# Decode attention with a gated feed-forward: the last weight loads cut into pieces of 4, 5, 2 and 1 blocks, the third split by partition

## The chip, the cores and the metric

The kernel runs on one core of a Trainium2 chip. The metric is device microseconds of one execution. One further execution was recorded by the hardware profiler, and all rows below are from that one.

## The reference, cut to what matters

```python
x = A_x                                            # [2, 1, 448]
g = sigmoid((x * gate_w).sum(-1, keepdims=True))
# attention for one new token: 16 heads of 256, 4096 cached keys, all float32
q = (x @ wq)  -> [2, 16, 1, 256]
p = softmax(q . k_cache * 256 ** -0.5)
a = (p . v_cache) -> [2, 1, 4096] @ wo             # wo: [4096, 448]
# feed-forward
h = relu(x @ w1 + b1) ** 2                         # w1: [448, 1792]
b = h @ w2 + b2                                    # w2: [1792, 448]
return g * a + (1 - g) * b                         # [2, 1, 448]
```

The caches k and v are 128 MiB each, and w2 is 1792 x 448 float32, 3.2 MB.

## The kernel before, in words

Work goes in 16 rounds. A round is one batch row and two heads; its keys are two loads of 4 MB (`load_k`), its values one load of 8 MB (`load_v`, L148). VectorE multiplies the keys by q (`times_q`, L305) and sums rows (`row_sums`, L310); TensorE multiplies the softmax weights with the values (`values`, L355). Keys, the last half of the values and all weights share a ring of three SBUF slots (tag `ring`), and the other values use one wide slot. All large loads are issued by SyncE (SP), in program order, on one DMA queue; a load into a slot waits until the last reader of the tile before it is done. The schedule is manual: each engine keeps the order in which the program is written.

w2 is viewed as `w2_v`, 128 partitions of 14 blocks (`FC`) of 448 float32, so that a partition's 14 blocks lie one behind the other in DRAM and a block is 1,792 bytes of one partition. The first two blocks (`WH`) are loaded early. The other 12 go into the ring's slot that the last half of the last keys leaves (`load_w2_late`), as the last loads of the program. Before the change they are four loads, cut at `W2_CUTS = (4, 8, 11)`: pieces of 4, 4, 3 and 1 blocks, each over all 128 partitions.

The end of the program, as TensorE executes it: the last values (`va`, then three pieces of `vb`), `take` and `turn` of the last two heads, `late_w2(0, 4)` with the first piece, `late_wo` of two heads (L405), then `late_w2(4, 12)` with the pieces left. A block of w2 is four matmuls in `late` (L401), in the trace eight records; they add up in the PSUM tile `fin`. ScalarE copies `fin` to `y4` (L504), and two small stores, one issued by SP (L506) and one by ScalarE (L507), write the output of 4 rows each.

The small loads at the start are issued by ScalarE: `x2`, `gw` and `b2r` of 2 rows each, and `b1T` of 128 rows.

Of the kernel before, what the change touches and what calls it, by code (L numbers as in the profile page):

```python
# [16 lines left out]
def kernel(  # L17
# [14 lines left out]
    nc = tc.nc  # L32
    P = 128
# [17 lines left out]
    assert QB == 2 * DH  # L51
    DQ = D // 4
    WH = 2
    W2_CUTS = (4, 8, 11)
    V_CUTS = (48, 56)
    LEAD = 4
    LEAD2 = 16
# [32 lines left out]
    w2_v = w2.rearrange("(p c) n -> p c n", c=FC)  # L90
    w2_sb = {}

    def w2_slot(lo, hi):
        t = slot(f"w2_{lo}")
        tv = t[:, :(hi - lo) * D].rearrange("p (c n) -> p c n", n=D)
        for c in range(lo, hi):
            w2_sb[c] = tv[:, c - lo, :]
        return tv
# [5 lines left out]
    def load_w2_late():  # L104
        tv = w2_slot(WH, FC)
        at = [0, *W2_CUTS, FC - WH]
        for lo, hi in zip(at, at[1:]):
            nc.sync.dma_start(tv[:, lo:hi, :], w2_v[:, WH + lo:WH + hi, :])

# [259 lines left out]
    def turn(u):  # L371
        n = len(units[u])
        pt = ps.tile([P, 512], F32, name=f"ot{u}", tag="sm")
        wide = n == HG
        nj = HJ if wide else NJ
        if wide:
            ov = o_w.rearrange("r s j k p -> r s j (k p)")
        else:
            ov = o_sb[u].rearrange("r (s p j) -> r s j p", s=2, j=nj)
        ptv = pt[:, :nj * n * B].rearrange("p (j c) -> p j c", c=n * B)  # L380
        for j in range(nj):
            for s in range(2):
                nc.tensor.matmul(ptv[:, j, :], ov[:, s, j, :], rl_t[u][:, :, s], start=(s == 0), stop=(s == 1))  # L383
        if wide:

            oT[u] = work.tile([P, HJ, B], F32, name=f"oT{u}", tag="oTw")
            for k in range(n):
                at = slice(k * HP, (k + 1) * HP)
                nc.scalar.activation(oT[u][at], ptv[at, :, B * k:B * k + B], AF.Copy)  # L389
        else:  # L390
            oT[u] = work.tile([P, NJ, n * B], F32, name=f"oT{u}", tag=f"oT{n}")
            nc.scalar.activation(oT[u], ptv, AF.Copy)
# [10 lines left out]
    def late_wo(h):  # L403
        u, k = unit_of[h]
        for j in range(NJ):  # L405
            late(oT[u][:, j, B * k:B * k + B], wo_sb[NG - 1][:, h % HG, j, :])

    def late_w2(lo, hi):
        for c in range(WH + lo, WH + hi):
            late(hT[:, c, :], w2_sb[c], stop=(c == FC - 1))  # L410
# [17 lines left out]
    for i, (b, n) in enumerate(rounds):  # L428
# [15 lines left out]
        if i == last:  # L444
            load_w2_late()
# [52 lines left out]
    turn(NG)  # L498
    late_w2(0, W2_CUTS[0])
    late_wo(H - 2)  # L500
    late_wo(H - 1)
    late_w2(W2_CUTS[0], FC - WH)
    y4 = const.tile([P, DQ], F32, name="y4")
# [31 lines left out]
```

## Time and profile before

| | us |
|---|---|
| median of 3 runs (lowest, highest) | 682.23 (681.94, 682.29) |
| the profiled execution, its own time | 682.01 |
| its span, first to last instruction | 680.2 |

The span covers 3,769 instructions. By its page DMA moves 289.79 MB at a mean of 426 GB/s, VectorE is busy for 571.7 us (84% of the span) and TensorE for 242.5 us (36%). The own time is 1.8 us above the span.

### The profile page before, as it was taken

Reading aid. Unit: us, or ns where it says so; the run is one execution under the profiler, and the core shown is the slowest. Engines: PE = TensorE matmul, PEld = TensorE weight load, DVE = VectorE, ACT = ScalarE, POOL = GpSimd, SP = SyncE. Lnnn points to the kernel's source line nnn. Section 1 sums busy time; section 2 is a strip of 40 time slices with the busy share of each in tenths; the row PEclk is TensorE's granted clock in tenths of the full one; section 3 lists DMA queues with packets and bytes.
Section 4 is the critical chain, followed back from the end, with each engine's and each line's share of the span. In section 5 each row is a group of like instructions: output and inputs, shape, how many; then the busy total and the mean of one; then the engine's idle time right before and its main releaser. Section 6 shows DMA issues by size and latency. Waiting matters only on the chain.

```text
span 680.2 us, 3769 instructions
## 1 busy us (share of the span) xinstructions
PE 242.5 (36%) x1618; PEld 85.2 (13%) x1618; DVE 571.7 (84%) x171; ACT 35.5 (5%) x110; POOL 0.7 (0%) x6
## 2 busy tenths in 40 slices
PE   2500506208158050504028450320506814033356
PEld 1100101005014010101004110000101400001013
DVE  3199999597987979799895979979796897999960
ACT  0100000100001000000001000000001000001000
POOL 0000000000000000000000000000000000000000
PEclk9955856758566685756657875575857757557779
DMA  9999999999999999999999999999999999999996
GB/s 379 436 459 414 429 461 405 448 418 426 456 405 455 407 431 443 421 447 418 445 419 436 449 413 447 416 447 418 444 438 411 449 422 432 446 414 430 413 430 265
DMA packets 9644, 289.79 MB, mean 426 GB/s; under 512 B 1174, under 2 KB 1308, under 8 KB 2332
## 3 DMA queue, kind: packets, MB, share of 16 engines
q1 hardware_dynamic: 9464, 289.54, 99.0%
q8 instruction: 12, 0.20, 0.1%
q10 hardware_dynamic: 164, 0.02, 0.0%
q14 instruction: 4, 0.03, 0.0%
HBM read 289.56 MB, written 0.00 MB: 426 GB/s over the span
## 4 chain that ended last, share of the span: by engine, by line
DMA 56%; DVE 26%; PE 17%; ACT 1%; issue 0%; SPq 0%; ACTq 0%
DMA v<-in_A_v_cache_dram 46%; PE po_buf L355 13%; DVE k L305 13%; DVE s L310 13%; DMA k<-in_A_k_cache_dram 4%; DMA wq<-in_A_wq_dram 3%; DMA w<-in_B_w_dram 3%; PE po_buf L225 1%; PE acc L396 1%; PE ot L383 1%; ACT shared L365 0%; PE fin L401 0%; ACT oT L389 0%; PE pq L262 0%; ACT qs L251 0%
## 5 line engine op out<-in xcount | busy, mean ns | idle before, releaser
L305 DVE TENSOR_TENSOR k<-k,q 128x4096 f32<-128x4096 f32 (+3 forms) x63 | 281.6, 4486 | 78.2 <-DMA k<-in_A_k_cache_dram 59.2
L310 DVE TENSOR_REDUCE s<-k 128x32 f32<-128x8192 f32 x32 | 278.0, 8686 | 1.1
L355 PE MATMUL po_buf<-v,pw 128*16 128x512 f32 (+1 forms) x960 | 137.2, 735 | 159.2 <-DMA v<-in_A_v_cache_dram 159.2
L318 PE MATMUL mt<-ident,m 128*64 128x64 f32 x64 | 7.3, 316 | 236.9 <-DVE m L314 236.9
L355 PEld LDWEIGHTS po_buf<-v,pw 128*16 128x16 f32 (+1 forms) x960 | 30.7, 111 | 254.2 <-issue 205.4
L318 PEld LDWEIGHTS mt<-ident,m 128*64 128x64 f32 x64 | 4.8, 190 | 244.4 <-issue 201.5
L329 ACT ACTIVATE pw<-s,nb 64x64 f32<-64x64 f32 x32 | 11.1, 348 | 275.0 <-DVE nb L324 274.7
L396 PE MATMUL acc<-wo,oT 128*2 128x448 f32 x48 | 23.4, 651 | 2.5 <-ACT oT L389 2.5
L383 PE MATMUL ot<-rl,shared 128*128 128x8 f32 x96 | 20.3, 350 | 5.2 <-ACT shared L365 5.2
L383 PEld LDWEIGHTS ot<-rl,shared 128*128 128x128 f32 x96 | 19.7, 314 | 8.3 <-ACT shared L365 8.3
L265 ACT ACTIVATE q<-pq 128x256 f32<-128x256 f32 x16 | 6.1, 384 | 196.0 <-PE pq L262 195.9
L262 PE MATMUL pq<-qs,ident 128*64 128x256 f32 x64 | 10.7, 419 | 0.7 <-ACT qs L251 0.7
L225 PE MATMUL po_buf<-wq,xT 128*4 128x512 f32 x56 | 8.3, 761 | 4.9 <-DMA wq<-in_A_wq_dram 4.9
L365 ACT ACTIVATE shared<-po_buf 128x1024 f32<-128x1024 f32 x6 | 5.8, 1020 | 55.8 <-PE po_buf L355 55.8
L286 PEld LDWEIGHTS pt<-ident,shared 4*128 4x128 f32 x28 | 6.9, 336 | 0.9 <-issue 0.9
L286 PE MATMUL pt<-ident,shared 4*128 4x4 f32 x28 | 7.0, 380 | 0.0
L396 PEld LDWEIGHTS acc<-wo,oT 128*2 128x2 f32 x48 | 4.4, 96 | 19.3 <-issue 16.5
L329 ACT ACTIVATION_READ_ACCUMULATOR pw<-s,nb 64x1 f32 x32 | 5.9, 185 | 0.0
L335 PE MATMUL sum<-rs,ones_pp 128*128 128x8 f32 (+1 forms) x10 | 3.0, 369 | 8.1 <-ACT pw L329 8.1
L355 PE MATMUL po_buf<-va,pw 128*8 128x512 f32 x32 | 5.2, 804 | 1.0 <-DMA va<-in_A_v_cache_dram 1.0
L225 PE MATMUL ph<-w,xT 128*4 128x448 f32 x28 | 5.4, 539 | 0.0
L262 PEld LDWEIGHTS pq<-qs,ident 128*64 128x64 f32 x64 | 3.3, 138 | 11.6 <-issue 9.7
(64 smaller groups left out, 60.8 us busy)
## 6 DMA issues: line engine op xcount, KB each, us to landing
k<-in_A_k_cache_dram SPq DMA_DIRECT2D x32, 4096.0 KB, 30.9
v<-in_A_v_cache_dram SPq DMA_DIRECT2D x2, 4096.0 KB, 28.9
wq<-in_A_wq_dram SPq DMA_DIRECT2D x1, 7168.0 KB, 19.7
wo<-in_A_wo_dram SPq DMA_DIRECT2D x4, 1792.0 KB, 34.0
va<-in_A_v_cache_dram SPq DMA_DIRECT2D x1, 4096.0 KB
w<-in_B_w_dram SPq DMA_DIRECT2D x1, 3136.0 KB
vb<-in_A_v_cache_dram SPq DMA_DIRECT2D x1, 2048.0 KB
vb<-in_A_v_cache_dram SPq DMA_DIRECT2D x2, 1024.0 KB, 16.8
```

The costliest lines, as they stand in the source:

```text
L225: nc.tensor.matmul(out[32 * g:32 * g + 2 * B, :width], xT[:, half, c].rearrange("p s b -> p (s b)"), t[:, (a * n + g) * width:(a * n + g + ...
L262: nc.tensor.matmul(pq[k * PH:(k + 1) * PH, :DH], ident[:, r:r + 1].to_broadcast([P, PH]), qs[:, k * DH:(k + 1) * DH], start=True, stop=True)
L265: nc.scalar.activation(q_sb[i], pq[:, :DH], AF.Copy)
L286: nc.tensor.matmul(pt[:, c, :], hv[:, c, :], ident[:2 * B, :2 * B], start=True, stop=True)
L305: nc.vector.tensor_tensor(kt, kt, q_sb[i].unsqueeze(1).to_broadcast([P, hi - lo, DH]), op=ALU.mult)
L310: nc.vector.tensor_reduce(s_t[i][:, half * J:(half + 1) * J], kts[i, half], axis=AX.X, op=ALU.add)
L318: nc.tensor.matmul(mt[at, :PH], m.to_broadcast([P, PH]), ident[:, at], start=True, stop=True)
L329: nc.scalar.activation(pw[k, b][at, :, 2 * c:2 * c + 2], s_t[i][at].rearrange("p (m s) -> p m s", s=2), AF.Exp, bias=nb[at], accum_out=rs_ ...
L355: nc.tensor.matmul(po[r:r + 4 * n, :], pw[k, b][:, m, :4 * n], vt[:, 2 * m:2 * m + 2, :].rearrange("p j d -> p (j d)"), start=(k == 0 and ...
L365: nc.scalar.activation(o_w[:, s], po_bufs[u % 2][:, s * DH:(s + 1) * DH].rearrange("r (p j) -> r j p", j=HJ).unsqueeze(2).to_broadcast([P, ...
L383: nc.tensor.matmul(ptv[:, j, :], ov[:, s, j, :], rl_t[u][:, :, s], start=(s == 0), stop=(s == 1))
L396: nc.tensor.matmul(acc[:, :D], oT[g][:, j, :], wo_sb[g][:, j, :], start=False, stop=(g == NG - 2 and j == HJ - 1))
```

## The change

The cuts become (4, 9, 11): pieces of 4, 5, 2 and 1 blocks. The third piece is issued as three loads that differ in their partitions: 0 to 63, 64 to 114 and 115 to 127, which is 64, 51 and 13 partitions. All bytes stay the same; six loads are issued where there were four. The order of TensorE's work is not touched.

```diff
     WH = 2
-    W2_CUTS = (4, 8, 11)
+    W2_CUTS = (4, 9, 11)
+    W2_ROWS = (64, 115)
     V_CUTS = (48, 56)
...
         at = [0, *W2_CUTS, FC - WH]
         for lo, hi in zip(at, at[1:]):
-            nc.sync.dma_start(tv[:, lo:hi, :], w2_v[:, WH + lo:WH + hi, :])
+            rows = [0, *(W2_ROWS if lo == W2_CUTS[1] else ()), P]
+            for p, e in zip(rows, rows[1:]):
+                nc.sync.dma_start(tv[p:e, lo:hi, :], w2_v[p:e, WH + lo:WH + hi, :])
```

## Rows read from the trace of the kernel before

**Rows 1.** The page: DMA packets in sum, and the chain that ended last.
```profile
DMA packets 9644, 289.79 MB, mean 426 GB/s; under 512 B 1174, under 2 KB 1308, under 8 KB 2332
...
DMA 56%; DVE 26%; PE 17%; ACT 1%; issue 0%; SPq 0%; ACTq 0%
```

**Rows 2.** The chain that ended last, from 655 us: start us, us, what.
```profile
647.50 8.70 DVE s L310
...
656.59 0.43 SPq L108
...
657.07 18.76 DMA w<-in_B_w_dram
...
675.87 0.99 PE fin L401 x32
...
676.89 0.26 ACT y L504
```

**Rows 3.** Windows at the end: us, busy by engine, clock, share of 16 DMA engines, GB/s.
```profile
670.00:672.00 2.00, 1.67 (x28) 0.84 (x20) 0.00 (x0) 0.60 (x1) 0.00 (x0) 1.00 1.02 419
672.00:672.50 0.50, 0.50 (x6) 0.50 (x5) 0.00 (x0) 0.00 (x0) 0.00 (x0) 1.00 0.94 384
672.50:673.00 0.50, 0.50 (x21) 0.48 (x24) 0.00 (x0) 0.18 (x1) 0.00 (x0) 1.00 0.93 369
673.00:673.50 0.50, 0.50 (x32) 0.50 (x24) 0.00 (x0) 0.00 (x0) 0.00 (x0) 1.00 0.70 283
673.50:674.00 0.50, 0.50 (x32) 0.50 (x24) 0.00 (x0) 0.00 (x0) 0.00 (x0) 1.00 0.62 226
674.00:674.50 0.50, 0.50 (x32) 0.40 (x24) 0.00 (x0) 0.00 (x0) 0.00 (x0) 1.00 0.45 179
674.50:675.00 0.50, 0.50 (x28) 0.33 (x16) 0.00 (x0) 0.00 (x0) 0.00 (x0) 1.00 0.29 100
675.00:675.50 0.50, 0.10 (x5) 0.00 (x0) 0.00 (x0) 0.00 (x0) 0.00 (x0) 1.00 0.23 79
675.50:676.00 0.50, 0.13 (x8) 0.13 (x12) 0.00 (x0) 0.00 (x0) 0.00 (x0) 1.00 0.16 61
676.00:676.50 0.50, 0.50 (x28) 0.50 (x24) 0.00 (x0) 0.00 (x0) 0.00 (x0) 1.00 0.00 0
```

**Rows 4.** DMA from 673 to 676 us: packets, MB, share of 16 engines.
```profile
q8 instruction: 1, 0.02, 2.3%
```

**Rows 5.** Timeline of the end: start us, us, engine, line, operation (xcount), idle before.
```profile
672.60 0.95 PE L401 MATMUL fin<-w,hT 128*2 128x112 f32 x32
...
673.37 0.95 PE L401 MATMUL fin<-wo,oT 128*2 128x112 f32 x32
...
674.15 0.95 PE L401 MATMUL fin<-w,hT 128*2 128x112 f32 x32
...
675.87 0.95 PE L401 MATMUL fin<-w,hT 128*2 128x112 f32 x32 [0.77 <-DMA w<-in_B_w_dram]
```

**Rows 6.** The page's DMA queues: packets, MB, share of 16 engines.
```profile
q1 hardware_dynamic: 9464, 289.54, 99.0%
q8 instruction: 12, 0.20, 0.1%
q10 hardware_dynamic: 164, 0.02, 0.0%
```

**Rows 7.** DMA of the first 30 us: queue packets; issues xcount, KB each.
```profile
q10 hardware_dynamic: 156, 0.02, 0.4%
...
x<-in_A_x_dram ACTq DMA_DIRECT2D x1, 3.5 KB
gw<-in_gate_w_dram ACTq DMA_DIRECT2D x1, 3.5 KB
b2r<-in_B_b_dram ACTq DMA_DIRECT2D x1, 3.5 KB
b1T<-in_B_b_dram ACTq DMA_DIRECT2D x1, 7.0 KB
```

**Rows 8.** SP's issues in the timeline from 630 us.
```profile
651.09 1.28 SPq L158 DMA_DIRECT2D vb<-in_A_v_cache_dram  x3
656.22 1.75 SPq L108 DMA_DIRECT2D w<-in_B_w_dram  x4
```

**Rows 9.** What SP's queue waited for, from 640 us: total us, times, longest.
```profile
SPq L506 <- ACT y L504: 12.3, 1, 12.3
SPq L506 <- DMA vb<-in_A_v_cache_dram: 6.8, 1, 6.8
```

## The prediction

> **What bounds the kernel now.** I read the page first, then the chain backwards from the end, then the DMA engines in half microseconds around the place where the chain leaves the loads. DMA moves 426 GB/s over the whole span and holds 56% of the chain [rows 1]. All loads before the late w2 keep their order, so everything up to SP's first w2 issue at 656.22 stays. The reader should look at the last piece of the chain: SP issues the third w2 piece at 657.07, its load holds the chain for 18.76 us and lands at 657.07 + 18.76 = 675.83, TensorE starts on it at 675.87, ScalarE copies at 676.89 [rows 2]. So the end hangs on when that piece lands on the slowest of 16 DMA engines.
>
> The windows show that "slowest" matters. Up to 672 the share is 1.02, all engines busy; then it falls over almost 4 us: 0.94, 0.93, 0.70, 0.62, 0.45, 0.29, 0.23, 0.16 [rows 3]. In engines that is 15 at 672 and 0.29 x 16 = 4.6 around 674.75, 3.7 around 675.25. The last window holds 0.16 x 0.5 x 16 = 1.28 engine-us: four engines that work until about 675.8. The sum of the eight shares times 0.5 is 2.16 us, so the same bytes spread evenly would be through at 674.16, 1.7 us earlier. An even finish is thus worth at most 1.7 us, 0.25% of the run, before TensorE's own work is counted.
>
> One reason for the spread is in the rows: one engine fetched instructions in this stretch, 2.3% of 16 engines over 3 us, 1.1 us of one engine [rows 4]; there are 12 such fetches in the span [rows 6]. As the load queue never runs dry, an engine that carried one or two stays late.
>
> **The change part by part.**
>
> *Unit.* At 419 GB/s one engine moves 26.2 GB/s [rows 3]; a block of one partition (1,792 B) takes 0.0684 us. A load over 128 partitions gives each engine 8 rows.
>
> *How the split loads fall on engines.* On the queue of the small loads the page counts 164 packets [rows 6], and the first 30 us hold 156 [rows 7]. Three loads of 2 rows and one of 128 are 134 rows, which leaves 22 = 2 + 2 + 2 + 16: one closing packet for each engine used. The other 8 packets are ScalarE's store of 4 rows: 4 rows and 4 closers, so 4 engines. So rows were dealt in equal shares over as many engines as that allows. For 64 partitions that is 16 engines with 4 rows; for 13 it is 13 with 1; for 51 it is 3 with 17. No row shows an odd count, so I bound 51 rows from both sides: all on one engine, or spread over 16 at 3 or 4 each. I take three, the nearest to the rows' equal shares.
>
> The Trainium skill ("DMA: Bandwidth & Descriptors", section "Why a DMA increments its semaphore by 16 and not by 1") says so outright: as many engines, up to 16, as divide the row count, and on this path the lowest-numbered ones, so 51 rows burden engines 0 to 2. The trace agrees for 2, 4 and 128 rows; no row here shows 51 or 13.
>
> *Work per engine in units (rows x blocks).* Through the third piece, before: 8 x 11 = 88; through the fourth, 96. After, the first two pieces are 8 x 9 = 72. The third adds 2 x (4 + 17 + 1) = 44 on the three engines, 2 x 5 = 10 on ten others, 2 x 4 = 8 on the last three. Through the third piece that makes 116, 82 and 80: +28, -6 and -8 units, or +1.92, -0.41 and -0.55 us. The same differences hold through the fourth.
>
> *Landings, if the three are early engines.* For a late engine of the ten, the third piece lands at 675.83 - 0.41 = 675.42. Before, the fourth landed at about 675.83 + 8 x 0.0684 = 676.38, which nothing waited for: TensorE reached block 11 only three blocks after 675.87. After, it lands at 675.97. The second piece had landed by 674.15, where TensorE starts on it without a wait [rows 5]; with one more block it lands by 674.15 + 0.55 = 674.70.
>
> *TensorE.* Groups of four blocks start 0.77 and 0.78 us apart and end 0.95 after their start [rows 5]: 0.193 a block and 0.18 for the last to drain. From a landing to the start take 0.04 (675.83 to 675.87). Three ways to the end: from the second piece, 674.74 + 8 x 0.193 + 0.18 = 676.46; from the third, 675.46 + 3 x 0.193 + 0.18 = 676.22; from the fourth, 676.01 + 0.193 + 0.18 = 676.38. The second piece, now five blocks, is the latest. Before, the end was 675.87 + 0.95 = 676.82. Gain: 0.36 us. A landing before 674.15 for the second piece would stop the gain at 0.44, where the fourth takes over. So the 1.93 us moved onto three engines buys a third of a microsecond: TensorE's queue of eight blocks behind the second piece is what shuts off the rest.
>
> *Two more issues, and a wait.* Four issues took 1.75 us [rows 8], so two more cost some 0.9 us of SP, from 657.97 to 658.9. SP also holds issues back for older loads: after 657.97 the output store, which reads no v, waited 6.8 us for a vb load, to 664.8 [rows 9]. I count the store as the eighth issue behind the first vb piece (two vb, four w2, one store on ScalarE's queue, then this). With two more loads, the eighth behind it is the fourth w2 piece: it would go out at 664.8 to 665.2 instead of 657.5. Behind it on SP stands only the store, which has to wait for y until 677.2 anyway. The cover is the engines' backlog: all stay busy to 672, 6.8 us after the issue [rows 3]; I cost it at nothing. Without the cover each microsecond late would be a microsecond at the end.
>
> *Waiting for three loads instead of one* in front of block 9: bounded by nothing and by one more instruction on TensorE's queue, below 0.04 us; I take nothing.
>
> *Sum.* 682.01 own time - 0.36 = 681.65. The median shown lies 0.22 above that execution's own time, so 681.87; I write 681.9. A difference of 0.2% (1.36 us) is about what a measurement of this kernel can tell from no change; this one is 0.05%.
>
> **The rivals.**
>
> *A. One of the three engines is late.* An engine that takes 17 rows ends 1.92 us later. If it is one of the four late ones, the fourth piece lands at 676.38 + 1.92 = 678.30, TensorE ends at 678.30 + 0.04 + 0.37 = 678.71, 1.89 later than before: 684.1, slower by 0.28%. It decides from the point where the engine's fourth piece landed, before, later than 676.82 - 0.41 - 1.92 = 674.49 (no gain left), and by 0.2% from 675.85 on. For it: dealt blindly, three engines miss the four late ones in 12 x 11 x 10 / (16 x 15 x 14) = 39% of cases. Against it: by 674 some half of the engines are through, and following the packet records from one packet's end to the next one's start, the two engines that carried the 2-row loads at the start are in the early half at the end (no view names engines, so this is a reading without a row, and the third engine stays open). Late engine 6%; one of the middle, between 682.3 and 683.6, 10%.
>
> *B. 51 rows on one engine.* It would carry 2 x (4 + 51 + 1) = 112 units in the third piece, or 2 x 68 = 136 if the 13 rows land there too, where it had 24; with the 8 more of the second piece that is 96 to 120 units on top, 6.6 to 8.2 us. Even an engine whose fourth piece landed at 673.5 would land it at 680.1 to 681.7; TensorE would end at 680.5 to 682.1, 3.7 to 5.3 later than before: 686 to 687.5. Rows for equal shares in 2, 4 and 128 don't exclude it. 3%.
>
> *C. The change doesn't do what it says.* If 51 rows spread over 16 engines, each has 8 to 9 rows again, the fourth piece lands at 676.38 as before, TensorE now waits for it: 676.38 + 0.04 + 0.37 = 676.79, and the time stays at 682.2. The same comes out if loads of 64 partitions run at half speed: 4 rows of 2 blocks take 0.55 us more, which eats the 0.41. The Trainium skill speaks for that ("SBUF — State Buffer", section "Door 1: The DMA port swizzle"): 64 adjacent partitions reach 8 of 16 ports, so such a load gets little more than half the speed. By it the fourth piece would land at 676.5 and the time be 682.3. No row here has a load of 64 partitions; against it stands that the late engines are alone at the end. Together 14%.
>
> **How the numbers follow.** Forecast (three early engines, 681.3 to 682.1 with the spread of 0.35 us among the runs shown) 65%; C 14%, 682.0 to 682.5; A's middle 10%, to 683.6; A late 6%, 684.1; B 3%, 686 to 687.5; 2% for a gain above 1.36 us, which needs more than the even finish leaves. The range from 681.2 to 683.1 takes in the forecast, C and most of A's middle. Faster by over 0.2%: 2%. Within 0.2% (680.9 to 683.6): 65 + 14 + 10 = 89%. Slower: 6 + 3 = 9%.
>
> **What would show it.** Right: six w2 issues, the last at about 665; the DMA share near 0.9 until about 674, then a steeper fall that ends near 675.4; TensorE's last group starting before 675.87 with less than 0.2 us of waiting on w2; y at about 676.5. Wrong in distribution: share of 0.06 to 0.2 lasting beyond 676 (one to three engines with the 17 rows), TensorE waiting there. Wrong in the queue: a DMA share falling below 1 before 671, because the fourth piece was issued too late.

## The result: 0.3% slower

The changed kernel takes 684.4 us (median of 8 runs) against 682.32 for the kernel before, a ratio of 1.0031 (95% interval 1.0019 to 1.0042). Forecast was 681.9, in a range from 681.2 to 683.1. The first profiled execution of the changed kernel ran its matmuls slower (TensorE busy for 378.2 us against 240.0) and took 703.88 us, so the ratio leaves it out, and the rows here are of a second profiled execution, whose own time of 684.80 us is its series' median (run `x1_again` below).

The end of the chain, as in [rows 2] (start us, us, what), and the timeline of TensorE there, as in [rows 5]:

```profile
656.43 20.76 DMA w<-in_B_w_dram
677.19 0.04 issue
677.24 2.58 PE fin L404 x64
679.82 0.02 issue
679.84 0.26 ACT y L507
```
```profile
672.68 0.95 PE L404 MATMUL fin<-w,hT 128*2 128x112 f32 x32
673.45 0.95 PE L404 MATMUL fin<-wo,oT 128*2 128x112 f32 x32
677.24 2.56 PE L404 MATMUL fin<-w,hT 128*2 128x112 f32 x64 [2.84 <-DMA w<-in_B_w_dram]
```

The piece that comes too late is not the split one. The load issued at 656.43 is the second, whole piece; it lands at 677.19, where the forecast had 674.70. TensorE idles for 2.84 us, and then its eight blocks take 2.56 us instead of 1.72.

The windows, as in [rows 3] (us, busy by engine, granted clock, share of 16 DMA engines, GB/s; a packet counts whole in the window in which it starts, so a share can come out above 1):

```profile
670.00:671.00 1.00, 1.00 (x20) 0.35 (x17) 0.00 (x0) 0.00 (x1) 0.00 (x0) 1.00 1.04 434
671.00:671.50 0.50, 0.31 (x16) 0.05 (x4) 0.00 (x0) 0.50 (x1) 0.00 (x0) 1.00 0.99 366
671.50:672.00 0.50, 0.35 (x3) 0.35 (x4) 0.00 (x0) 0.10 (x1) 0.00 (x0) 1.00 1.07 244
672.00:672.50 0.50, 0.50 (x7) 0.50 (x6) 0.00 (x0) 0.00 (x0) 0.00 (x0) 1.00 1.03 254
...
673.50:674.00 0.50, 0.50 (x32) 0.50 (x24) 0.00 (x0) 0.00 (x0) 0.00 (x0) 1.00 0.95 219
...
676.50:677.00 0.50, 0.00 (x0) 0.00 (x0) 0.00 (x0) 0.00 (x0) 0.00 (x0) 1.00 0.42 129
677.00:677.50 0.50, 0.26 (x12) 0.27 (x16) 0.00 (x0) 0.00 (x0) 0.00 (x0) 1.00 0.34 129
677.50:678.00 0.50, 0.50 (x31) 0.50 (x24) 0.00 (x0) 0.00 (x0) 0.00 (x0) 0.93 0.12 43
678.00:678.50 0.50, 0.50 (x20) 0.45 (x15) 0.00 (x0) 0.00 (x0) 0.00 (x0) 0.50 0.00 0
...
679.50:680.00 0.50, 0.30 (x8) 0.00 (x0) 0.00 (x0) 0.16 (x1) 0.00 (x0) 0.50 0.00 0
```

Read the last two columns together. Until 671 they say 434 GB/s at a share of 1.04, 26 GB/s for each busy engine. From 671.5 the engines stay busy but move 244 GB/s at 1.07, 14 GB/s each. Before, a falling share and falling GB/s went together [rows 3]; here engines are busy and slow. The column before them, the granted clock, falls from 1.00 to 0.50 (2.4 to 1.2 GHz) at about 678, while TensorE is at work again.

### The profile page after: what moved, and what is told of

Read it like the earlier page. It is cut to its first block, busy times and chain, and to the rows that moved or that the text cites. A ratio compares the mean times of both kernels' runs of the same rounds, so it can differ in the third digit from the quotient of the medians.

```text
span 702.0 us, 3772 instructions
## 1 busy us (share of the span) xinstructions
PE 378.2 (54%) x1618; PEld 103.7 (15%) x1618; DVE 571.6 (81%) x171; ACT 35.4 (5%) x110; POOL 0.7 (0%) x6
## 4 chain that ended last, share of the span: by engine, by line
DMA 52%; PE 36%; DVE 10%; ACT 1%; issue 0%; ACTq 0%
DMA v<-in_A_v_cache_dram 49%; PE po_buf L358 32%; DVE k L308 5%; DVE s L313 5%; DMA wq<-in_A_wq_dram 3%; PE po_buf L228 2%; PE fin L404 1%; PE ot L386 1%; PE pq L265 0%; ACT pw L332 0%; ACT q L268 0%; PE sum L338 0%; ACT o L372 0%; ACT qs L254 0%; DVE nb L327 0%
## 5 line engine op out<-in xcount | busy, mean ns | idle before, releaser
L358 PE MATMUL po_buf<-v,pw 128*16 128x512 f32 (+1 forms) x960 | 225.5, 1140 | 122.3 <-DMA v<-in_A_v_cache_dram 120.6
L358 PEld LDWEIGHTS po_buf<-v,pw 128*16 128x16 f32 (+1 forms) x960 | 39.2, 140 | 281.8 <-issue 235.6
L399 PE MATMUL acc<-wo,oT 128*2 128x448 f32 x48 | 39.4, 1023 | 2.5 <-ACT oT L392 2.5
L386 PE MATMUL ot<-rl,shared 128*128 128x8 f32 x96 | 22.8, 373 | 4.9 <-ACT shared L368 4.9
L386 PEld LDWEIGHTS ot<-rl,shared 128*128 128x128 f32 x96 | 22.3, 349 | 10.9 <-ACT shared L368 10.9
L265 PE MATMUL pq<-qs,ident 128*64 128x256 f32 x64 | 17.3, 669 | 0.7 <-ACT qs L254 0.7
L228 PE MATMUL po_buf<-wq,xT 128*4 128x512 f32 x56 | 13.1, 1134 | 4.8 <-DMA wq<-in_A_wq_dram 4.8
L228 PE MATMUL ph<-w,xT 128*4 128x448 f32 x28 | 11.6, 1030 | 0.0
L358 PE MATMUL po_buf<-vb,pw 128*8 128x512 f32 x32 | 8.0, 1152 | 0.0
L358 PE MATMUL po_buf<-va,pw 128*8 128x512 f32 x32 | 7.5, 1124 | 0.0
```

What stands on the lines that cost most here:

```text
L228: nc.tensor.matmul(out[32 * g:32 * g + 2 * B, :width], xT[:, half, c].rearrange("p s b -> p (s b)"), t[:, (a * n + g) * width:(a * n + g + ...
L265: nc.tensor.matmul(pq[k * PH:(k + 1) * PH, :DH], ident[:, r:r + 1].to_broadcast([P, PH]), qs[:, k * DH:(k + 1) * DH], start=True, stop=True)
L358: nc.tensor.matmul(po[r:r + 4 * n, :], pw[k, b][:, m, :4 * n], vt[:, 2 * m:2 * m + 2, :].rearrange("p j d -> p (j d)"), start=(k == 0 and ...
L399: nc.tensor.matmul(acc[:, :D], oT[g][:, j, :], wo_sb[g][:, j, :], start=False, stop=(g == NG - 2 and j == HJ - 1))
```

## The experiments

Each is the file of the changed kernel or the one before with the edit shown; "..." marks lines left out. The ratio is to runs of the kernel before on the same chip.

**The changed kernel again, for its profile.**

> The changed kernel once more, for a profile at the usual TensorE clock. Theory L (one of the three DMA engines that take 17 rows is late, by fetched instructions, so the loads end on it): 1.5 to 2.2 us slower than before; one engine alone is busy at the end, a DMA share of about 0.06 for over half a microsecond, and TensorE waits for w2 in front of its last group. Theory P (a load of 64 partitions runs at about half speed on every engine): slower too, but the share stays at 0.2 or more until the end, several engines ending together. Theory Q (the fourth piece is issued late, behind an older load's landing): a DMA share that drops below 0.9 before 671 and comes back.

684.80 us, ratio 1.0037 (1.0023 to 1.0051), 2.5 us slower. Theory L, rival A of the forecast, comes near in size (1.5 to 2.2 us) and has the wrong picture: the share is 0.42 at 676.75, six to seven engines, not one. Theory Q is out, since the share stays at 1 until 672.5. The rows look most like P's: the share is still 0.34 from 677 to 677.5.

**The cuts alone.**

```diff
-    W2_ROWS = (64, 115)
+    W2_ROWS = ()
```

> Cuts 4, 5, 2, 1 alone, every piece over all 128 partitions. All three theories: no loss. The fourth piece now has two blocks in front of it instead of three, so 0.0 to 0.4 us faster to 0.3 us slower than before (worked out: second piece at 674.7, third 675.83, fourth 676.38, TensorE's end 676.79 against 676.82).

682.43 us, 1.0001 (0.9992 to 1.0009): the cuts neither cost nor gain anything that can be measured. The loss is in the split. The second piece, the same five blocks, lands at 675.02 here:

```profile
656.62 18.40 DMA w<-in_B_w_dram
675.02 0.04 issue
```

**The split alone.**

```diff
-    W2_CUTS = (4, 9, 11)
+    W2_CUTS = (4, 8, 11)
```

> Old cuts 4, 4, 3, 1 with the third piece, now three blocks, in loads of 64, 51 and 13 partitions. Theory L: the 17 rows are half as long again, three engines get 42 units more than before instead of 28, 2.9 us instead of 1.9: about 1.0 us slower than the changed kernel, 2.5 to 3.2 us slower than before. Theory Q: same number of loads and waits, so the same time as the changed kernel. Theory P: the 64 rows cost 0.8 instead of 0.55 us more, so some 0.3 us slower than the changed kernel.

685.67 us, 1.0051 (1.0039 to 1.0064), 0.9 us above the changed kernel. Q is out again; L (1.0) fits better than P (0.3), which stays.

**Two halves, no 51 and 13.**

```diff
-    W2_ROWS = (64, 115)
+    W2_ROWS = (64,)
```

> Cuts 4, 5, 2, 1 with the third piece in two loads of 64 partitions each; no engine carries more rows than another. Theory L: no loss, within 0.3 us of the cuts alone. Theory P: 0.5 to 1.1 us slower than the cuts alone, since all of the third piece goes through loads of 64 partitions. Theory Q: within 0.3 us of the cuts alone.

685.11 us, 1.0040 (1.0027 to 1.0052). No engine carries more rows than another, yet the loss is as large as the changed kernel's. That ends L as the main cause: the loads of 51 and 13 aren't needed for the loss. It is also more than twice what P was sized at: 2.7 us above the cuts alone instead of 0.5 to 1.1. TensorE waits twice here, for the second piece and then for the split one, and its last three blocks take 1.30 us, where 3 x 0.193 + 0.18 are 0.76:

```profile
676.67 1.14 PE L404 MATMUL fin<-w,hT 128*2 128x112 f32 x40 [2.20 <-DMA w<-in_B_w_dram]
678.82 1.30 PE L404 MATMUL fin<-w,hT 128*2 128x112 f32 x24 [1.01 <-DMA w<-in_B_w_dram]
```

**The same two halves, interleaved.** Two more theories now: S, that writing to one side of the partitions slows all engines; N, that it is the number of loads.

```diff
-            rows = [0, *(W2_ROWS if lo == W2_CUTS[1] else ()), P]
-            for p, e in zip(rows, rows[1:]):
-                nc.sync.dma_start(tv[p:e, lo:hi, :], w2_v[p:e, WH + lo:WH + hi, :])
+            if lo == W2_CUTS[1]:
+                parts = [slice(0, P, 2), slice(1, P, 2)]
+            else:
+                parts = [slice(0, P)]
+            for at_p in parts:
+                nc.sync.dma_start(tv[at_p, lo:hi, :], w2_v[at_p, WH + lo:WH + hi, :])
```

> As the two halves, but the two loads of 64 partitions take every second one (0, 2, 4 and so on, then 1, 3, 5), so number, size and engines' shares of the loads stay and only the partitions differ. Theory S (a load that stays on one side, partitions 0 to 63 or 64 to 127, slows every engine that runs beside it): no loss, within 0.4 us of the cuts alone, and the share stays paired with 25 GB/s or more for each busy engine. Theory N (two or three loads with few rows for each engine cost by their number): 2.5 to 3 us slower than before, as the two halves.

682.28 us, 0.9996 (0.9987 to 1.0005). Two loads of 64 partitions cost nothing if each takes every second partition. Three windows of each, the halves first and then the interleaved ones:

```profile
671.50:672.00 0.50, 0.28 (x3) 0.29 (x3) 0.00 (x0) 0.16 (x1) 0.00 (x0) 1.00 1.08 233
672.00:672.50 0.50, 0.50 (x6) 0.50 (x6) 0.00 (x0) 0.00 (x0) 0.00 (x0) 1.00 0.87 219
672.50:673.00 0.50, 0.50 (x15) 0.48 (x18) 0.00 (x0) 0.14 (x1) 0.00 (x0) 1.00 1.01 240
```
```profile
671.50:672.00 0.50, 0.40 (x4) 0.40 (x4) 0.00 (x0) 0.04 (x1) 0.00 (x0) 1.00 1.00 409
672.00:672.50 0.50, 0.50 (x6) 0.50 (x6) 0.00 (x0) 0.00 (x0) 0.00 (x0) 1.00 0.98 401
672.50:673.00 0.50, 0.50 (x18) 0.48 (x21) 0.00 (x0) 0.18 (x1) 0.00 (x0) 1.00 0.87 348
```

The share is alike, the rate differs by a factor of about 1.5 to 1.8.

**Interleaved 64, then 51 and 13.** The edit is against the interleaved halves.

```diff
-                parts = [slice(0, P, 2), slice(1, P, 2)]
+                parts = [slice(0, P, 2), slice(1, 103, 2), slice(103, P, 2)]
```

> As the changed kernel, but the 64 partitions are the even ones, and the 51 and 13 are the odd ones up to 101 and from 103. Theory S: within 0.5 us of the cuts alone, faster if the three engines with 17 rows are early ones. Theory L of the first runs (the 17 rows themselves are the loss): 1.5 to 2.2 us slower than before. Theory N: as the changed kernel, 2 to 3 us slower.

682.59 us, 1.0003 (0.9994 to 1.0011). With the rows spread over both sides, unequal loads of 51 and 13 rows neither cost nor gain anything that can be measured. The sign is still there, but fainter: 333 GB/s at a share of 1.09 from 672 to 672.5.

**TensorE kept at work in the wait.**

```diff
+    dm = ps.tile([P, 512], F32, name="dm", tag="pq")
+    for _ in range(12):
+        nc.tensor.matmul(dm[:16, :], ident[:, :16], qs, start=True, stop=True)
     late_w2(W2_CUTS[0], FC - WH)
```

> The changed kernel with 12 matmuls of 512 columns into a tile that nobody reads, ahead of the last w2 matmuls, in the stretch where TensorE waited 2.84 us for w2. If the fall of the granted clock to half during the last group belongs to the loss: the last 64 records take 1.7 to 1.9 us instead of 2.56, 0.6 to 0.8 us faster than the changed kernel in its slower runs and no run above 684.3. If the clock plays no part: the same as the changed kernel, and slower by what the 12 matmuls exceed the wait.

691.61 us, 1.0133 (1.0119 to 1.0147). A miss in size: eight records of `values` take 1.04 us, but 23 records of these take 10.03 us. The wait was overfilled, and the time says nothing about the clock. With `range(3)`:

> The busy wait again with 3 matmuls of 512 columns, sized by the first one (23 records took 10.03 us, so 6 records take 2.6 us): they end at about 676.8, before the second w2 piece lands at 677.2. If the fall of the granted clock belongs to the loss: no fall, the last 64 records take 1.7 to 2.1 us instead of 2.56, median 683.8 to 684.2, and no run above 684.6. If not: 684.8 as the changed kernel, runs up to 685.5.

684.01 us, 1.0025 (1.0015 to 1.0035), and its eight runs lie between 683.67 and 684.21, where the changed kernel's five lie between 683.78 and 685.50. The granted clock stays at 1.00, and the group takes 1.77 us:

```profile
674.13 2.74 PE L507 MATMUL dm<-qs,ident 128*16 128x512 f32 x6
676.80 1.77 PE L404 MATMUL fin<-w,hT 128*2 128x112 f32 x64
```

So the clock's fall is up to 0.8 us of the loss (2.56 against 1.77). That it also makes the changed kernel's runs spread fits, but is not shown: none of its faster runs was profiled. Not all of the 1.1 us between the two profiled executions is the clock's, since here the second piece had landed by 676.80, 0.4 us earlier.

**32, 64 and 32 partitions.**

```diff
-    W2_ROWS = (64, 115)
+    W2_ROWS = (32, 96)
```

> The third piece in loads of partitions 0 to 31, 32 to 95 and 96 to 127; the middle one has 64 adjacent partitions, half on each side. Theory S: half of the rows go through one-sided loads instead of all, so about half of the loss of the two halves, 1.0 to 1.8 us slower than before. Theory N: three loads, so at least the loss of the two halves, 2.5 to 3.5 us.

683.11 us, 1.0009 (1.0000 to 1.0018): 0.8 us, somewhat below what S gave (1.0 to 1.8) and far below N's 2.5 to 3.5.

**Keys on one side, in the middle of the kernel before.**

```diff
-        nc.sync.dma_start(t, of_round(k_cache, i)[:, half * J:(half + 1) * J, :])
+        cuts = (0, PH, P) if (i, half) == (6, 0) else (0, P)
+        for p, e in zip(cuts, cuts[1:]):
+            nc.sync.dma_start(t[p:e], of_round(k_cache, i)[p:e, half * J:(half + 1) * J, :])
```

> The kernel before, with one load of 4 MB of keys (round 6, first half) cut into two loads, partitions 0 to 63 and 64 to 127; the tail is not touched. Theory S: while these 4 MB move, all engines are busy at about half the rate, 200 to 240 GB/s, for some 18 us instead of 9.8, so 7 to 10 us slower than before. Theory N (number of loads): one load more, within 0.5 us of before.

695.31 us, 1.0193 (1.0179 to 1.0207): one load of 4 MB cut in two costs 13 us of 682. S had the rate right, but expected 7 to 10 us. The windows of this stretch, of the cut keys and then of the kernel before:

```profile
248.00:252.00 4.00, 0.71 (x5) 0.20 (x4) 2.51 (x1) 0.38 (x1) 0.00 (x0) 1.00 0.96 197
252.00:256.00 4.00, 0.00 (x0) 0.00 (x0) 4.00 (x1) 0.00 (x0) 0.00 (x0) 0.57 1.05 221
256.00:260.00 4.00, 0.00 (x0) 0.00 (x0) 3.97 (x2) 0.00 (x0) 0.00 (x0) 0.50 0.86 180
260.00:264.00 4.00, 0.00 (x0) 0.00 (x0) 4.00 (x1) 0.00 (x0) 0.00 (x0) 0.50 1.20 246
```
```profile
248.00:252.00 4.00, 0.00 (x0) 0.00 (x0) 4.00 (x1) 0.00 (x0) 0.00 (x0) 0.76 1.08 467
252.00:256.00 4.00, 0.00 (x0) 0.00 (x0) 4.00 (x1) 0.00 (x0) 0.00 (x0) 0.50 1.20 516
256.00:260.00 4.00, 0.00 (x0) 0.00 (x0) 3.97 (x2) 0.00 (x0) 0.00 (x0) 0.50 0.83 360
260.00:264.00 4.00, 0.00 (x0) 0.00 (x0) 4.00 (x1) 0.00 (x0) 0.00 (x0) 0.50 1.02 442
```

The mean of the four is 211 against 446 GB/s, 47%, with the engines as busy. For 4 MB alone that is 19.9 instead of 9.4 us, 10.5 more; the slow stretch lasts longer than these four windows, with 246 GB/s from 264 to 268 and 295 at a share of 0.72 from 268 to 272.

**Another uneven split: 119 and 9 partitions.** The second piece gets the split, to take work off the late engines earlier.

```diff
-    W2_CUTS = (4, 9, 11)
-    W2_ROWS = (64, 115)
+    W2_CUTS = (4, 6, 10)
+    W2_ROWS = (119,)
...
-            rows = [0, *(W2_ROWS if lo == W2_CUTS[1] else ()), P]
+            rows = [0, *(W2_ROWS if lo == W2_CUTS[0] else ()), P]
```

> Pieces of 4, 2, 4 and 2 blocks, the second in loads of 119 partitions (if rows are dealt in equal shares, 17 rows on each of 7 engines) and 9 partitions (one row on 9 engines). Engines without these rows have 16 units less before the last pieces, 1.1 us; the seven have 20 more, 1.4 us. If the seven are the early ones and their rows, spread over both sides, don't slow the others: the last landing at 675.3 instead of 676.3, 0.4 to 0.9 us faster than before. If rows of 17 adjacent partitions on one engine slow the others as the loads of 64 do: 0.3 to 1.5 us slower.

And its control, the kernel before with `W2_CUTS = (4, 6, 10)` and no split:

> Pieces of 4, 2, 4 and 2 blocks, each over all partitions: what stands beside the loads of 119 and 9. The last piece has two blocks of matmuls behind its landing at 676.38 instead of one: within 0.3 us of before under every theory.

686.25 us, 1.0055 (1.0041 to 1.0069), against 682.72, 1.0011 (1.0002 to 1.0020), for the control, which itself is 0.5 us above the kernel before instead of within 0.3. The split costs 3.5 us; against the kernel before it is 4.0, where 0.3 to 1.5 was the most expected. Its windows show the same picture, 254 GB/s at a share of 1.03, beside 423 at 1.04 for the control:

```profile
670.00:671.00 1.00, 0.81 (x8) 0.22 (x12) 0.00 (x0) 0.00 (x0) 0.00 (x0) 1.00 1.03 254
```
```profile
670.00:671.00 1.00, 1.00 (x16) 0.36 (x20) 0.00 (x0) 0.00 (x0) 0.00 (x0) 1.00 1.04 423
```

Some 1.1 of the 3.5 us is the clock, 0.50 from 679 on: the last six blocks take 2.42 us, where 6 x 0.193 + 0.18 are 1.34. These rows reach both sides, so "one side" is not all of it: runs of 17 adjacent partitions on seven engines slow the others too. Which of these engines meet where was not tried.

**Written side or read side.** In all of these the adjacent partitions in SBUF were also adjacent rows in DRAM. Two kernels part them, for the same 4 MB of keys; both leave these keys in partitions other than their scores need.

```diff
-        nc.sync.dma_start(t, of_round(k_cache, i)[:, half * J:(half + 1) * J, :])
+        src = of_round(k_cache, i)[:, half * J:(half + 1) * J, :]
+        if (i, half) == (6, 0):
+            for n in range(2):
+                nc.sync.dma_start(t[n * PH:(n + 1) * PH], src[n:P:2])
+        else:
+            nc.sync.dma_start(t, src)
```

> As the keys cut into loads of 64, but the two loads write adjacent partitions (0 to 63, 64 to 127) from every second row of DRAM; the 4 MB of keys thereby stand in other partitions than their scores need, the work stays the same. Theory SD (the side written in SBUF is what slows): the loss of the one-sided keys again, 12 to 14 us, with 200 to 215 GB/s while they move. Theory SR (the side read in DRAM): no loss, within 0.7 us of before.

```diff
...
+            for n in range(2):
+                nc.sync.dma_start(t[n:P:2], src[n * PH:(n + 1) * PH])
...
```

> The reverse: the two loads read adjacent rows of DRAM and write every second partition; again these keys stand in other partitions than their scores need. Theory SD: no loss, within 0.7 us of before. Theory SR: 12 to 14 us slower.

Adjacent in SBUF: 694.56 us, 1.0185 (1.0168 to 1.0202). Adjacent in DRAM: 682.35 us, 1.0001 (0.9992 to 1.0010). One window of each, in this order:

```profile
248.00:252.00 4.00, 0.33 (x4) 0.00 (x0) 0.98 (x1) 0.38 (x1) 0.00 (x0) 0.95 0.97 197
```
```profile
248.00:252.00 4.00, 0.00 (x0) 0.00 (x0) 3.97 (x1) 0.28 (x1) 0.00 (x0) 0.84 0.97 418
```

The partitions written decide it; which rows are read played no measurable part here.

## Why the prediction was wrong, by its own steps

*How the split loads fall on engines* held. The page of the changed kernel has 16 packets more than before [rows 6] on SP's queue:

```profile
q1 hardware_dynamic: 9480, 289.54, 98.8%
```

The number of rows is the same. Four loads over 16 engines had 64 closing packets; six have 16 + 16 + 16 + 16 for the whole ones and the 64, and 16 left for the 51 and the 13: 3 + 13. The trace's records of landings, one for each engine of a load (no view prints them), say it outright: three for the one, 13 for the other. This is what the rule of the Trainium skill ("DMA: Bandwidth & Descriptors", section "Why a DMA increments its semaphore by 16 and not by 1") gives, and the count rules out rival B and 51 rows over 16 engines.

*Two more issues, and a wait* held: the issues waited for older loads, twice where the forecast had one wait, and this cost nothing that can be measured. SP's issues and what its queue waited for:

```profile
656.06 9.18 SPq L111 DMA_DIRECT2D w<-in_B_w_dram  x6
```
```profile
SPq L111 <- DMA vb<-in_A_v_cache_dram: 4.6, 1, 4.6
...
SPq L111 <- DMA va<-in_A_v_cache_dram: 1.9, 1, 1.9
```

The last issue ends at 665.24, with the engines busy for 7 us more. The interleaved 64, 51 and 13 have as many issues, the last near 665 too, and took 682.59 us.

*Landings* is the step that failed. It priced every row at 0.0684 us a block, wherever the row is written, and so the second piece, whose only change was one block more, at 674.70. It landed at 677.19, 2.49 us later; some 0.3 of that isn't the split's, as the cuts alone landed it at 675.02. By the records of landings the first piece lands on its first engine at 668.72 and on its last at 672.34. The second piece follows on its first engine after 2.74 us, as priced, but on its last only after 4.85 us, where with the cuts alone it is 2.70. The load of partitions 0 to 63 has landed on its first engine at 672.33, so the late engines still write the second piece while the early ones are in the split loads. *TensorE* then failed by the clock, for which the forecast had no term: 0.18 + 8 x 0.193 = 1.72 us became 2.56, 0.84 more. The two explain the end: forecast 676.46, measured 677.24 + 2.56 = 679.80, 3.34 later, and 2.50 + 0.84 = 3.34.

Rival C had named the mechanism and mis-sized it. It took half speed as a cost of the load's own rows, 0.55 us on each engine, and held that the late engines are alone at the end. They weren't: from 671.5 to 672.5 the engines move 14 to 15 GB/s each, and the slow stretch reaches those that still work on the second, whole piece. With the halves, where nothing else is uneven, the loss against the cuts alone is 2.7 us, some 0.5 of it the clock's, instead of the 0.5 to 1.1 that half speed for their own rows gives. So the 14% went to no change instead of a loss.

The rule that spoke against the change was the Trainium skill's ("SBUF — State Buffer", section "Door 1: The DMA port swizzle"): partitions 0 to 63 reach 8 of 16 ports. The trace agrees: 47% of the rate for the one-sided keys, none lost when interleaved, only the written side counts, and a middle load over both sides costs less. What it doesn't settle is the load of 119, which reaches both sides; that 17 adjacent partitions on each of seven engines put several of them on one port at a time is only argued.

Rival A's time, 684.1, came close to the measured 684.4 by luck, since the loss has another reason. With the rows spread over both sides, the 17 rows on three engines cost no measurable time. That instruction fetches are what makes some engines late was argued, and no run tests it.

The even finish itself never got a fair test above noise: the best without clashes, the interleaved halves, stays within 0.1% of before, and no version here is measurably faster than the kernel before.

## What to carry to other kernels

Cut a load along its free dimension, not into adjacent partitions; if rows must be split, let each load take every second partition. When the end of a DMA-bound kernel is late, read share and GB/s together: in these runs a falling share was engines out of work, and a full share at about half the GB/s came with loads into adjacent partitions, and then pieces that were not touched were late too. A wait in front of TensorE's last work can cost twice, as it did here, once as the wait and once in the clock behind it.

## What the runs showed of the hardware that was not expected

One load of 4 MB, cut into two of 64 adjacent partitions in the middle of the stream, cost 13 us: the loads behind it in the queue wait, and the 8 MB of values issued at 246.71 landed 43.34 us later, against 31.22 before. The granted clock fell from 1.00 to 0.50 at about 678, with TensorE at work again after its wait of 2.84 us, and stayed there to the end of its work; with six matmul records in the wait, 2.74 us of them, it stayed at 1.00 and the last group took 1.77 us.
